# Placing the feature-tile sum of a projection in a later step of a fused spectral and attention kernel

## The chip, the cores and the metric

The kernel runs on one core of one Trainium2 chip. The metric is the device time of one execution in microseconds (us), the median of several runs; the profile comes from one execution of its own. Engines are named as in the profile: PE is TensorE (PEld its weight loads), DVE is VectorE, ACT is ScalarE, POOL is GpSimd, SP issues most of the DMAs.

## The reference

Four layers, each added to a residual of 2048 rows by 512 columns, each behind a layer norm: a Fourier mixing layer (real part of a transform along the hidden axis and then along the sequence), an attention layer with memory, and the same two again. The attention layer has 32 heads of 16 columns and goes over the sequence in four segments of 512 rows:

```python
phi = lambda t: jnp.where(t > 0, t + 1.0, jnp.exp(t))
for s in range(N):
    qs, ks, vs = q[:, :, s], k[:, :, s], v[:, :, s]
    logits = jnp.einsum("bhqd,bhkd->bhqk", qs, ks) * scale + mask
    p = _softmax(logits, axis=-1)
    a_dot = jnp.einsum("bhqk,bhkd->bhqd", p, vs)
    pq = phi(qs)
    num = jnp.einsum("bhld,bhde->bhle", pq, M)
    den = jnp.einsum("bhld,bhd->bhl", pq, z)[..., None] + 1e-6
    a_mem = num / den
    o = g * a_mem + (1.0 - g) * a_dot
    outs.append(o)
    pk = phi(ks)
    M = M + jnp.einsum("bhld,bhle->bhde", pk, vs)
    z = z + jnp.einsum("bhld->bhd", pk)
```

So a feature tile `phi(q)` is wanted in segments 1 to 3 (to read the memory), and `phi(k)` in segments 0 to 2 (to add to it). The mask adds -1e9 where the key lies behind the query.

## The kernel before

The four layers are written as Python generators, one step of each at a time. `place(order, gen, slots...)` puts the steps of a generator on a list of slots; the program is then written slot by slot, within a slot by `order`. In an attention layer a unit is four heads of one segment, 32 units in all, and takes 10 slots; a group `g` is two units (20 slots), a segment four groups. Slot `b` is where a segment's first unit starts, `t` where a group's does.

What stands on an engine's queue is not simply that order. A scheduling layer below puts each engine's instructions in order by readiness and priority: TensorE's stay in the order written (`keep_in_program_order`), instructions under `tc.high_priority` go earlier, and `tc.issue_after(x)` (in the helper `after`) holds an instruction back behind `x` in that order. Waits between engines are then derived from the data.

The steps that matter here:

- `proj(s, g, n)` (from line 996) makes the projection of `q` or `k` of one group: 12 matmuls `pqk` in four steps. In the fourth, ScalarE copies the result to `praw` (line 1032), GpSimd splits off the bf16 parts (`parts` line 1033, `rem` line 1034), and `feature()` puts two ScalarE passes down, relu (line 1024) and exp (line 1025), into the tile `phi`. The next step is ScalarE's second part (line 1038) and, before the change, `feature_sum()`: one VectorE instruction (line 1029) that reads `praw` and `phi` in SBUF, 128x512 f32 each, and writes the finished `phi`. Then GpSimd's third part (line 1042) and the DMAs to DRAM. For groups 0 and 1 of segment 0 (`late`) both `feature()` and the sum come in a step of their own instead.
- `natural_max(s, g, u)` makes a unit's scores row by row (matmuls `nat<-stkk,stkq`) and reduces each to its maximum by one VectorE instruction and a read of its accumulator (line 1102, `junk` and `mx`): 32 pairs a unit, 1024 in the program, written with high priority. Lines 1118 to 1125 split the maxima into bf16 parts (`mparts`), which TensorE turns (`mT`).
- `softmax_values` makes the scores again transposed (`sT`), subtracts the maxima in the same matmul, and ScalarE applies relu and exp into `pT` (lines 1175 and 1176); GpSimd zeroes the future by a select (line 1181); `pv_bank` matmuls follow, and `output` scales them on VectorE (lines 1268 to 1288) and adds the memory's part on GpSimd (line 1286).
- `nat`, `sT`, `pqk`, `pvv`, `po` and the rest take their PSUM from one ring of seven banks (`bank`). A matmul that opens a bank waits for whoever read what was there seven banks earlier, which is VectorE for a bank of `nat`.
- `mem_read` (matmuls `pm`) and `mem_update` (transposes `pkT`) are the readers of `phi`. They stand on slots that come 17 or more behind the sum's step.

Where the steps stood:

```python
yield
A.activation(parts[:, 1], rem, AF.Copy)
if with_phi and not late:
    feature_sum()
yield
E.tensor_tensor(out=parts[:, 2], in0=rem, in1=parts[:, 1], op=ALU.subtract)
```

with the four steps of the matmuls on four slots `at`, and the rest on `post(at[3])`, the three slots behind the last of them.

Of the kernel before, what the change touches and what calls it, by code (L numbers as in the profile page):

```python
# [58 lines left out]
def spectral_infini_kernel(  # L59
# [11 lines left out]
    folded=None,  # L71
):
    nc = tc.nc
    V, A, G, T = nc.vector, nc.scalar, nc.gpsimd, nc.tensor
# [78 lines left out]
        G.tensor_tensor(out=r[:n], in0=ve[:n], in1=half_neg[:n], op=ALU.pow)  # L153
        return mv, ve, r

    first_row, opened, drained = [], [], []

    @contextmanager
    def after(what):
        with ExitStack() as all_:  # L160
            for i in what:
                all_.enter_context(tc.issue_after(i.ins))
            yield
# [36 lines left out]
    def place(order, gen, *at):  # L200
        for t in itertools.chain(*at):
            slots.setdefault(t, []).append((order, gen))
# [735 lines left out]
    def place_attention(x_in, x_out, t0, ws, w_at, out_at, last=None, final=False, turned=False):  # L938
# [59 lines left out]
        def proj(s, g, n):  # L998
            ps = bank("pqk")
            for d in range(DT):  # L1000
                matmul3(
                    ps,
                    lambda h: ws[n, d][:, h, g * P : (g + 1) * P],
                    lambda h: xT[s][:, h, d, :],
                    d == 0,
                    d == DT - 1,
                )
                if d + 1 < DT:
                    yield

            def phi_tile():
                if (s, g) not in phi:
                    phi[s, g] = pair("phi", "ut", 8, F32)
                return phi[s, g][:, "qk".index(n)]

            parts = sb.tile([P, 3, 512], BF16, name="parts", bufs=2)
            with_phi = (n == "q" and s > 0) or (n == "k" and s < NSEG - 1)
            late = s == 0 and g < 2
            rem = sb.tile([P, 512], F32, name="rem", bufs=1)
            raw = sb.tile([P, 512], F32, name="praw", bufs=2) if with_phi else rem  # L1020
            sign = -1.0 if n == "q" else 1.0

            def feature():
                A.activation(phi_tile(), raw, AF.Relu, scale=-sign)
                A.activation(phi_tile(), phi_tile(), AF.Exp, scale=-1.0)

            def feature_sum():
                op = (ALU.min, ALU.subtract) if n == "q" else (ALU.max, ALU.add)
                V.scalar_tensor_tensor(phi_tile(), raw, 0.0, phi_tile(), op0=op[0], op1=op[1])

            E = V if turned and (s, g) == (0, 0) else G
            A.activation(raw, ps, AF.Copy, scale=sign)
            E.tensor_copy(parts[:, 0], raw)
            E.tensor_tensor(out=rem, in0=raw, in1=parts[:, 0], op=ALU.subtract)
            if with_phi and not late:
                feature()
            yield
            A.activation(parts[:, 1], rem, AF.Copy)  # L1038
            if with_phi and not late:
                feature_sum()  # L1040
            yield
            E.tensor_tensor(out=parts[:, 2], in0=rem, in1=parts[:, 1], op=ALU.subtract)  # L1042
            yield
            sd = dram.tile([NSLOT, P, 512], BF16, name=f"scr{n}", bufs=3)
            dst = sd.rearrange("o p s -> p o s")
            o = 0
            for a, cnt, step in SLOTS[n]:
                src = parts[:, a : a + cnt] if step else parts[:, a : a + 1].to_broadcast(
                    [P, cnt, 512]
                )  # L1050
                nc.sync.dma_start(dst[:, o : o + cnt], src)
                o += cnt
            scr[s, g, n] = sd
            yield
            if with_phi and late:
                feature()
                feature_sum()
                yield

        def stack(s, g, u):  # L1060
# [19 lines left out]
        def natural_max(s, g, u):  # L1080
            qs, ks = stacks[s, g, u, "q"], stacks[s, g, u, "k"]
            mx = sb.tile([P, HU, LT], F32, name="mx", bufs=2)

            def scores(*cols):
                ps = bank("nat")
                views, off = [], 0
                for h, i in cols:
                    n = (i + 1) * P
                    T.matmul(
                        ps[:, off : off + n],  # L1090
                        qs[:KROWS, h, i * P : (i + 1) * P],
                        ks[:KROWS, h, :n],
                        start=True,
                        stop=True,
                    )
                    views.append((ps[:, off : off + n], mx[:, h, i : i + 1]))
                    off += n
                for src, dst in views:
                    n = src.shape[1]
                    junk = sb.tile([P, 512], BF16, name="junk", bufs=1)  # L1100
                    with tc.high_priority(offset=URGENT):
                        V.tensor_tensor_reduce(  # L1102
                            junk[:, :n], src, mask[:, 512 - n :], 1.0, 3e38,
                            ALU.add, ALU.min, dst,
                        )

            for h in range(HU):
                scores((h, 3))
                yield
                scores((h, 0), (h, 2))  # L1110
                yield
                if h % 2:
                    scores((h - 1, 1), (h, 1))
                    yield
            parts = max_parts[((s * NG + g) * (HG // HU) + u) % 2]
            rem = sb.tile([P, HU, LT], F32, name="mrem", bufs=2)
            with tc.high_priority(offset=2 * URGENT):
                V.scalar_tensor_tensor(
                    parts[:, 0], mx, -2.0, mx, op0=ALU.mult, op1=ALU.add
                )  # L1120
                for dst in rem, parts[:, 1]:
                    V.scalar_tensor_tensor(
                        dst, mx, -1.0, parts[:, 0], op0=ALU.mult, op1=ALU.subtract
                    )
                V.scalar_tensor_tensor(
                    parts[:, 2], rem, 1.0, parts[:, 1], op0=ALU.mult, op1=ALU.subtract
                )
            maxima[s, g, u] = parts
            yield
# [324 lines left out]
        def post(t):  # L1454
            return [t + 1, t + 2, t + 3]
# [6 lines left out]
        for n in range(NSEG * USEG):  # L1462
            t = t0 + SU * n
# [11 lines left out]
        for s in range(NSEG):  # L1475
# [27 lines left out]
            for g in range(NG):  # L1503
                t = b + SG * g
                late = [] if s or g > 1 else [b + 3 + 2 * g]
                at = {
                    (0, 0): [b - FOLD + 27 + k // 2 for k in range(8)] if turned else run_from(b - 34, 8),
                    (0, 1): run_from(b - 18, 8),
# [2 lines left out]
                    (1, 0): among(b - 40, b - 29, 8),  # L1511
                    (1, 1): among(b - 29, b - 17, 8),
                }.get((s, g), light(t - 50))
                place(2, proj(s, g, "q"), at[:4], post(at[3]))
                place(2, proj(s, g, "k"), at[4:], post(at[7]), late)
                if s > 0:
                    place(2, mem_read(s, g), [t - 12, t - 8])
                if s < NSEG - 1:
# [43 lines left out]
    else:  # L1562
# [11 lines left out]
        for t, (edge, other) in zip(folded.masks, ((0.0, 1.0), (0.0, -1.0))):  # L1574
# [15 lines left out]
            late=taken,  # L1590
# [210 lines left out]
```

## Time and profile before

| what | value |
|---|---|
| median of 3 runs | 1245.22 us (1245.03 to 1257.96) |
| time of the profiled execution | 1242.76 us |
| its span, first to last instruction | 1241.0 us |
| mean granted TensorE clock | 0.983 |
| PE busy | 1149.4 us, 93% |
| DVE busy | 952.8 us, 77% |
| ACT busy | 850.1 us, 68% |
| POOL busy | 433.8 us, 35% |
| sums of line 1029 | 48, 44.4 us in all |

The first attention layer fills the span from about 110 us to 620 us, the second from about 720 us on; the stretches before them are the Fourier layers. In a row of the timeline stand the start in us, the duration in us, engine, line, operation, what is written and read, and in brackets the idle time of the engine just before and what ended it. In a row of the waits stand who waited for whom, the total in us, how often, and the longest.

### The profile page before, as it was taken

The page shows a single profiled execution, that of the slowest core. Times are in us where ns is not written, and L with a number is a line of the kernel's source. Part 1 is how long each engine was busy: PE and PEld are TensorE (multiplying, and loading weights), DVE is VectorE, ACT ScalarE, POOL GpSimd, SP SyncE. Part 2 cuts the span into 40 slices and gives each one's busy share as a digit, 9 for nine tenths or more (in the row PEclk, how much of TensorE's full clock was granted, in tenths as well). Part 3 has the DMA queues.
Part 4 walks back from the last instruction along what each step waited for, and adds up shares of the span by engine and source line. Part 5 has one row for each costly group of instructions (what it writes and reads, how often), then busy time and mean ns, then how long its engine had stood idle before and what let it go on. Part 6 is the DMA issues. An engine that isn't in the chain of part 4 may idle for free.

```text
span 1241.0 us, 24436 instructions
## 1 busy us (share of the span) xinstructions
PE 1149.4 (93%) x7720; PEld 743.6 (60%) x7720; DVE 952.8 (77%) x3440; ACT 850.1 (68%) x1928; POOL 433.8 (35%) x750
## 2 busy tenths in 40 slices
PE   6989898998999999988989998899999999999897
PEld 5766455666655665545577764556666556655454
DVE  8788787778877877777697787877787778777772
ACT  5463487887787777886525426888777887878762
POOL 1111453433444444441110134454334443435200
PEclk9999898999999999998999998999999999999999
DMA  9596544435554454462428773543354444544411
GB/s 367 179 307 224 171 141 122 142 121 159 162 158 120 136 174 133 139 207 91 154 84 272 271 248 123 157 136 123 106 178 155 139 137 143 162 140 135 151 45 54
DMA packets 111125, 197.66 MB, mean 159 GB/s; under 512 B 13917, under 2 KB 63075, under 8 KB 110986
## 3 DMA queue, kind: packets, MB, share of 16 engines
q1 hardware_dynamic: 107722, 195.22, 49.0%
q8 instruction: 63, 1.03, 0.3%
q10 hardware_dynamic: 3264, 0.79, 0.3%
q14 instruction: 76, 0.62, 0.2%
HBM read 128.04 MB, written 67.14 MB: 157 GB/s over the span
## 4 chain that ended last, share of the span: by engine, by line
PE 61%; DVE 16%; DMA 7%; ACT 7%; issue 5%; POOL 3%; SPq 0%; ACTq 0%; DVEq 0%; POOLq 0%
PE pqk L85 11%; PE pv_bank L85 9%; PE sT L85 8%; PE nat L85 8%; DVE junk L1102 7%; PE u L85 5%; PE po L85 5%; PE pvv L85 5%; DMA chk<-in_chk 4%; ACT pT L1176 2%; PE pm L85 2%; PE pM L85 2%; PE on L85 1%; ACT sT L1175 1%; PE yr L85 1%
## 5 line engine op out<-in xcount | busy, mean ns | idle before, releaser
L1102 DVE CUSTOM_DVE_ANT_0 junk<-nat,mask 128x512 bf16<-128x512 f32 (+3 forms) x1024 | 500.2, 489 | 141.8 <-PE nat L85 108.2
L1176 ACT ACTIVATE pT<-sT 128x512 f32<-128x512 f32 x640 | 367.0, 598 | 45.0 <-PE sT L85 20.3
L1181 POOL TENSOR_SCALAR_AFFINE_SELECT pT<-pT 128x512 f32<-128x512 f32 x392 | 169.8, 446 | 404.0 <-ACT pT L1176 364.9
L85 PE MATMUL sT<-stkq,stkk 99*128 99x256 bf16 (+3 forms) x1024 | 250.4, 308 | 15.9 <-DVE mx L1102 9.8
L85 PE MATMUL nat<-stkk,stkq 96*128 96x512 bf16 (+3 forms) x1024 | 237.2, 303 | 20.4 <-DVE mx L1102 17.7
L1175 ACT ACTIVATE sT<-sT 128x256 f32<-128x256 f32 (+1 forms) x560 | 182.5, 335 | 55.7 <-PE sT L85 49.7
L85 PEld LDWEIGHTS <-stkk 99*128 99x128 bf16 x1024 | 83.2, 99 | 140.8 <-issue 125.5
L85 PE MATMUL pv_bank<-pT,vt 128*17 128x512 f32 (+3 forms) x2048 | 151.5, 434 | 0.0
L85 PEld LDWEIGHTS <-stkq 96*128 96x128 bf16 x1024 | 92.7, 99 | 65.8 <-issue 26.4
L85 PE MATMUL pqk<-xT,wq 128*128 128x512 f32 x384 | 126.2, 441 | 3.3 <-ACT xT L100 1.8
L85 PE MATMUL pqk<-xT,wk 128*128 128x512 f32 x384 | 126.6, 442 | 0.3
L85 PE MATMUL pvv<-wv,xT 128*128 128x512 f32 x384 | 122.0, 432 | 2.0 <-DVE mx L1102 2.0
L85 PE MATMUL po<-wo,oh 128*128 128x512 f32 x384 | 121.7, 435 | 2.2 <-DVE oh L102 1.4
L904 ACT ACTIVATE chk<-chk,reps 128x1024 f32<-128x1024 f32 (+1 forms) x80 | 81.4, 1022 | 40.1 <-DMA chk<-in_chk 39.8
L85 PEld LDWEIGHTS pv_bank<-pT,vt 128*17 128x17 f32 x2048 | 53.3, 97 | 79.4 <-issue 75.2
L1286 POOL TENSOR_TENSOR onat<-onat,otmp 128x128 f32<-128x128 f32 x96 | 48.5, 513 | 103.8 <-DVE otmp L1285 97.8
L1102 DVE DVE_READ_ACCUMULATOR2_ANT mx<- 128x1 f32 x1024 | 84.1, 82 | 0.0
L1042 POOL TENSOR_TENSOR parts<-rem,parts 128x512 bf16<-128x512 f32 x60 | 72.4, 1207 | 27.9 <-ACT parts L1038 23.1
L85 PEld LDWEIGHTS po<-wo,oh 128*128 128x128 f32 x384 | 68.6, 193 | 21.4 <-DVE oh L102 3.6
L85 PEld LDWEIGHTS pqk<-xT,wq 128*128 128x128 f32 x384 | 69.2, 191 | 16.2 <-ACT xT L100 2.3
L85 PEld LDWEIGHTS pqk<-xT,wk 128*128 128x128 f32 x384 | 68.8, 195 | 13.6 <-DVE mx L1102 1.0
L85 PEld LDWEIGHTS pvv<-wv,xT 128*128 128x128 f32 x384 | 67.4, 189 | 15.6 <-DVE mx L1102 4.5
(257 smaller groups left out, 1671.7 us busy)
## 6 DMA issues: line engine op xcount, KB each, us to landing
chk<-in_chk SPq DMA_DIRECT2D x68, 512.0 KB
stkq<-scrq SPq DMA_DIRECT2D x64, 384.0 KB
stkk<-scrk SPq DMA_DIRECT2D x64, 384.0 KB
scrq<-parts SPq DMA_DIRECT2D x32, 384.0 KB
scrk<-parts SPq DMA_DIRECT2D x32, 384.0 KB
mid<-xrm SPq DMA_DIRECT2D x32, 256.0 KB
scrq<-parts SPq DMA_DIRECT2D x32, 256.0 KB
scrk<-parts SPq DMA_DIRECT2D x32, 256.0 KB
```

What stands on the lines that cost most here:

```text
L85: return tc.keep_in_program_order(op(*args, **kwargs))
L904: A.activation(t[:, c : c + row], t[:, c : c + row], AF.Abs, bias=rep[:, col : col + 1], scale=scale, accum_out=acc[:, col : col + 1],)
L1042: E.tensor_tensor(out=parts[:, 2], in0=rem, in1=parts[:, 1], op=ALU.subtract)
L1102: V.tensor_tensor_reduce(junk[:, :n], src, mask[:, 512 - n :], 1.0, 3e38, ALU.add, ALU.min, dst,)
L1175: A.activation(blocks, blocks, AF.Relu)
L1176: A.activation(dst, ps, AF.Exp, scale=-SCALE)
L1181: G.affine_select(blocks, blocks, pattern=[[0, n] for n in blocks.shape[1:-1]] + [[1, P]], compare_op=ALU.is_ge, fill=0.0, base=0, channel ...
L1286: G.tensor_tensor(out=dst, in0=dst, in1=tmp, op=ALU.add)
```

## The change

The sum is taken out of the projection's fifth step and gets one of its own at the end, five slots behind the last matmuls (`end`) rather than one, for all 22 sums of an attention layer that are not `late`. In it, `after(last_max)` holds it behind the maximum that was written last at that point. `numerators` is declared and not used.

```diff
-    first_row, opened, drained = [], [], []
+    first_row, opened, drained, numerators, last_max = [], [], [], [], []
...
             A.activation(parts[:, 1], rem, AF.Copy)
-            if with_phi and not late:
+            if with_phi and not late and not folded:
                 feature_sum()
...
             if with_phi and late:
                 feature()
                 feature_sum()
+                yield
+            elif folded:
+                if with_phi:
+                    with after(last_max):
+                        feature_sum()
                 yield
...
-                        V.tensor_tensor_reduce(
+                        last_max[:] = [V.tensor_tensor_reduce(
                             junk[:, :n], src, mask[:, 512 - n :], 1.0, 3e38,
                             ALU.add, ALU.min, dst,
-                        )
+                        )]
...
+                end = lambda t: [t + 5] if turned and (s or g > 1) else []
...
-                place(2, proj(s, g, "q"), at[:4], post(at[3]))
-                place(2, proj(s, g, "k"), at[4:], post(at[7]), late)
+                place(2, proj(s, g, "q"), at[:4], post(at[3]), end(at[3]))
+                place(2, proj(s, g, "k"), at[4:], post(at[7]), end(at[7]), late)
```

The order of instructions on PE, ACT and SP is the same before and after. On POOL some of the additions of line 1286 stand behind one or two selects more. On DVE the 44 sums stand 6 to 20 rows further down, and some neighbours (`xn`, `xT`, `oh`, `xo`) trade places with a maximum. Behind line 1057 the lines of the changed kernel have numbers that are 5 higher, so its maxima are line 1107.

First place: VectorE's queue at the projection of `q` of the third group of segment 2 in the first attention layer (the sum that runs at 381 us in the profile). Before, the sum stands ahead of the pairs that follow it:

```order
L1029 SCALAR_TENSOR_TENSOR phi<-praw,phi 128x512
L1102 ISA junk,mx<-nat,mask 128x256
L1102 ISA mx 128x1
L1102 ISA junk,mx<-nat,mask 128x256
L1102 ISA mx 128x1
L1102 ISA junk,mx<-nat,mask 128x512
L1102 ISA mx 128x1
L1102 ISA junk,mx<-nat,mask 128x128
L1102 ISA mx 128x1
L1102 ISA junk,mx<-nat,mask 128x384
L1102 ISA mx 128x1
```

The same stretch now:

```order
L1107 ISA junk,mx<-nat,mask 128x256
L1107 ISA mx 128x1
L1107 ISA junk,mx<-nat,mask 128x256
L1107 ISA mx 128x1
L1107 ISA junk,mx<-nat,mask 128x512
L1107 ISA mx 128x1
L1107 ISA junk,mx<-nat,mask 128x128
L1107 ISA mx 128x1
L1107 ISA junk,mx<-nat,mask 128x384
L1107 ISA mx 128x1
L1029 SCALAR_TENSOR_TENSOR phi<-praw,phi 128x512
```

The sum went behind five maxima, ten rows.

Second place: the landing of the sum for `k` of the same group, before (the sum stood 15 rows higher):

```order
L1125 SCALAR_TENSOR_TENSOR mparts_75<-mrem,mparts_75 128x16
L1102 ISA junk,mx<-nat,mask 128x512
L1102 ISA mx 128x1
L1268 RECIPROCAL rec<-on 128x16
L1102 ISA junk,mx<-nat,mask 128x128
L1102 ISA mx 128x1
L1269 TENSOR_TENSOR rec<-rec,gate 128x16
```

and now:

```order
L1130 SCALAR_TENSOR_TENSOR mparts_75<-mrem,mparts_75 128x16
L1107 ISA junk,mx<-nat,mask 128x512
L1107 ISA mx 128x1
L1273 RECIPROCAL rec<-on 128x16
L1029 SCALAR_TENSOR_TENSOR phi<-praw,phi 128x512
L1107 ISA junk,mx<-nat,mask 128x128
L1107 ISA mx 128x1
L1274 TENSOR_TENSOR rec<-rec,gate 128x16
```

The sum now stands right ahead of a maximum, behind the reciprocal that scales the unit before.

Third place: the landing of the sum for `q` of segment 1's last group (it runs at 282 us before and stood 17 rows higher). Before:

```order
L1102 ISA junk,mx<-nat,mask 128x128
L1102 ISA mx 128x1
L1102 ISA junk,mx<-nat,mask 128x384
L1102 ISA mx 128x1
L177 TENSOR_SCALAR xn<-xt,norms,roots 128x512
L1102 ISA junk,mx<-nat,mask 128x512
```

and now:

```order
L1107 ISA junk,mx<-nat,mask 128x384
L1107 ISA mx 128x1
L1029 SCALAR_TENSOR_TENSOR phi<-praw,phi 128x512
L177 TENSOR_SCALAR xn<-xt,norms,roots 128x512
L1107 ISA junk,mx<-nat,mask 128x512
```

The sum now stands ahead of `xn`, a row of the next segment's normalised input.

## The prediction

> **What bounds the kernel now.** I read the page first, then who TensorE waits for, then the two attention layers as windows, and last the sums themselves. From the page, the span, the busy times and the chain that ended last:
>
> ```profile
> span 1241.0 us, 24436 instructions
> PE 1149.4 (93%) x7720; PEld 743.6 (60%) x7720; DVE 952.8 (77%) x3440; ACT 850.1 (68%) x1928; POOL 433.8 (35%) x750
> PE 61%; DVE 16%; DMA 7%; ACT 7%; issue 5%; POOL 3%; SPq 0%; ACTq 0%; DVEq 0%; POOLq 0%
> ```
>
> TensorE is the bound, and where the chain leaves it, it goes through VectorE more than twice as often as through ScalarE. TensorE's idle time is what a change that leaves its work alone can win. Its waits, over the whole span:
>
> ```profile
> PE nat L85 <- DVE mx L1102: 17.7, 35, 1.2
> PE sT L85 <- DVE mx L1102: 9.8, 18, 1.2
> PE on L85 <- ACT ot L1249: 6.3, 6, 1.8
> PE pM L85 <- DVE mx L1102: 3.5, 4, 0.9
> PE pvv L85 <- DVE mx L1102: 2.0, 6, 0.4
> ```
>
> The maxima (`mx`) end most of them: a matmul wants a bank of the ring whose maximum has not been taken. The first attention layer as one window (length, then busy time of each engine) shows how much there is:
>
> ```profile
> 150.00:600.00 450.00, 423.50 (x2996) 260.70 (x2995) 351.50 (x1405) 351.46 (x826) 185.35 (x321) 0.98 0.45 141
> ```
>
> TensorE is idle for 450.00 - 423.50 = 26.5 us there. VectorE has 98.5 us of idle time, so it is late only at places, not as a whole. The sums, as a line and as a group:
>
> ```profile
> L1029 DVE SCALAR_TENSOR_TENSOR phi<-praw,phi x48: 647/855/1640, 109.6 to 1141.6; 128x512 f32<-128x512 f32 x48
> L1029 DVE SCALAR_TENSOR_TENSOR phi<-praw,phi 128x512 f32<-128x512 f32 x48 | 44.4, 925 | 8.8 <-ACT phi L1025 8.3
> ```
>
> A sum takes 0.65 us at best, 1.64 at worst, and VectorE stands still for 8.3 us in all until ScalarE's exp is done. One of them from close by, in the order of time:
>
> ```profile
> 281.73 0.63 ACT L1025 ACTIVATE phi<-phi 128x512 f32<-128x512 f32 x1
> 281.95 1.16 POOL L1034 TENSOR_TENSOR rem<-praw,parts 128x512 f32<-128x512 f32 x1
> 282.38 1.28 DVE L1029 SCALAR_TENSOR_TENSOR phi<-praw,phi 128x512 f32<-128x512 f32 x1 [1.18 <-ACT phi L1025]
> 284.52 0.38 PE L85 MATMUL sT<-stkq,stkk 99*128 99x512 bf16 x1 [0.32 <-DVE mx L1102]
> 285.57 0.38 PE L85 MATMUL nat<-stkk,stkq 96*128 96x512 bf16 x1 [0.67 <-DVE mx L1102]
> 286.83 1.16 PE L85 MATMUL pM<-vt,pkn 128*128 128x136 f32 x8 [0.88 <-DVE mx L1102]
> ```
>
> VectorE waits 1.18 us for exp, then the sum takes 1.28, twice its best. The maxima queue behind it for 2.46 us, and TensorE stands still three times, 0.32 + 0.67 + 0.88 = 1.87 us, each time for a maximum.
>
> **What goes: the stalls at the old places.** I looked in the first layer for TensorE's waits within some 3 us behind each of the 22 sums that move, and kept those ended by VectorE. There are 16, in 9 places: the three above, the same three at 412.73, 413.77 and 415.03, and ten more, the first, some between and the last of which are, with the one left out at 186.97 and the last of the second layer,
>
> ```profile
> 185.55 0.38 PE L85 MATMUL sT<-stkq,stkk 99*128 99x384 bf16 x2 [0.65 <-DVE mx L1102]
> 186.97 0.38 PE L85 MATMUL nat<-stkk,stkq 96*128 96x256 bf16 x2 [0.80 <-DVE mx L1102]
> 323.40 0.38 PE L85 MATMUL nat<-stkk,stkq 96*128 96x128 bf16 x2 [0.46 <-DVE mx L1102]
> 384.07 0.97 PE L85 MATMUL pvv<-wv,xT 128*128 128x512 f32 x3 [0.36 <-DVE mx L1102]
> 510.99 0.97 PE L85 MATMUL pvv<-wv,xT 128*128 128x512 f32 x3 [0.36 <-DVE mx L1102]
> 540.31 0.97 PE L85 MATMUL po<-wo,oh 128*128 128x512 f32 x3 [0.22 <-DVE oh L102]
> 1144.79 0.96 PE L85 MATMUL po<-wo,oh 128*128 128x512 f32 x3 [0.23 <-DVE oh L102]
> ```
>
> By place they come to 0.65 + 1.87 + 0.86 + 0.36 + 1.87 + 0.22 + 0.28 + 0.36 + 0.46 = 6.9 us. (The 0.80 at 186.97 is that of an `xn` that stands between, and stays.) At each place what the sum holds VectorE for is more than the gap, so the whole gap can go. The second layer has the same waits 605 us later, the last at 1144.79 (0.23), so 13.8 us in all. Behind the other 13 sums that move TensorE waits for no maximum of theirs.
>
> **What comes: the sums at the new places.** A sum is now ready long before its turn, so the wait for exp goes, and each costs its own 0.65 to 1.64 us less the room there: VectorE's idle time up to the next maximum that a matmul is waiting for. At 16 of 22 places there is room enough, since VectorE waits for `nat` anyway. Two such places, where the sum now comes ahead of a maximum that had waited:
>
> ```profile
> 355.53 0.69 DVE L1102 CUSTOM_DVE_ANT_0 junk<-nat,mask 128x512 bf16<-128x512 f32 x1 [0.77 <-PE nat L85]
> 541.77 0.69 DVE L1102 CUSTOM_DVE_ANT_0 junk<-nat,mask 128x512 bf16<-128x512 f32 x1 [0.71 <-PE nat L85]
> ```
>
> At six places a layer there is little. As windows from the new place to that next maximum (length, PE, PEld, DVE busy):
>
> ```profile
> 190.07:193.28 3.21, 2.78 (x22) 1.92 (x20) 3.01 (x14) 3.21 (x10) 0.95 (x2) 1.00 0.05 12
> 290.08:292.38 2.30, 1.99 (x14) 1.54 (x13) 2.07 (x5) 2.30 (x6) 1.55 (x3) 1.00 0.42 147
> 298.91:300.05 1.14, 0.91 (x7) 0.59 (x6) 1.14 (x8) 1.14 (x5) 0.15 (x1) 1.00 0.54 205
> 331.95:333.07 1.12, 1.12 (x6) 0.43 (x5) 1.11 (x6) 0.73 (x4) 0.62 (x2) 1.00 0.00 0
> 391.58:392.53 0.95, 0.95 (x5) 0.43 (x5) 0.94 (x7) 0.04 (x1) 0.00 (x0) 1.00 1.02 370
> 418.29:420.35 2.06, 1.98 (x14) 1.55 (x13) 1.82 (x4) 1.93 (x5) 1.32 (x2) 1.00 0.19 66
> ```
>
> VectorE's idle time in them is 0.20, 0.23, 0, 0.01, 0.01 and 0.24, together 0.69 us. Six sums at 0.65 cost 3.90 - 0.69 = 3.2 us a layer; six at 1.64 cost 9.84 - 0.69 = 9.2. I take the short price. The long one is that of a sum beside GpSimd's part of a projection:
>
> ```profile
> 292.23 1.16 POOL L1042 TENSOR_TENSOR parts<-rem,parts 128x512 bf16<-128x512 f32 x1 [0.75 <-ACT parts L1038]
> 292.30 1.64 DVE L1029 SCALAR_TENSOR_TENSOR phi<-praw,phi 128x512 f32<-128x512 f32 x1
> 418.29 1.16 POOL L1034 TENSOR_TENSOR rem<-praw,parts 128x512 f32<-128x512 f32 x1
> 418.53 1.21 DVE L177 TENSOR_SCALAR xn<-xt,norms,roots 128x512 f32<-128x512 f32 x1 [0.23 <-PE xnT L85]
> ```
>
> The sum at 292.30 ends 0.55 us after GpSimd's instruction does, as does the one at 282.38. Four of the six places have at most short selects beside them. At the other two, ahead of `xn` (290.08 and 418.29), `rem` runs, but there `xn` waits for it already, so a sum that waits out the same instruction adds its own 0.55 to 0.65 rather than the wait once more.
>
> The Trainium skill, page “SBUF — State Buffer”, section “Who interferes with whom”, says that a VectorE instruction with two inputs in SBUF and a GpSimd one that reads SBUF shut each other out for a whole instruction, whoever comes first. The trace agrees (1.64 us beside a GpSimd instruction of 1.16). By the rule the new places are no safer than the old where a later `rem` has just begun, so it speaks against the change; a sum would then cost up to 1.16 + 0.65 = 1.81 us, an estimate, and six of them 10.2 us a layer.
>
> Costed at nothing: the bookkeeping of `last_max` issues no instruction. The later end of `phi` is covered by the 17 slots or more to its readers, of which the move takes four; were that gone, `pm` or `pkT` would wait. `praw` has two buffers and is kept four slots longer; the next projection that wants the same one is a whole projection further. The queues of SP and ACT keep their order, and the additions on GpSimd (line 1286) that trade places with selects have 65% of idle time on that engine about them.
>
> **The sum.** 13.8 - 2 x 3.2 = 7.4 us of TensorE's idle time go. Not all of it reaches the end: a TensorE that is earlier meets what is late next, and that is ScalarE (`on <- ot` above, and its share of 7% in the chain). I take the ratio of the chain, 7 of 7 + 16, for what is given back: 30%, leaving 5.2 us. Against the profiled execution's own 1242.8 that is 1237.6; the median of the runs shown is 2.4 us higher, 1245.2, so I forecast **1240 us**.
>
> **The rivals.**
>
> *Given back whole* (1245 us). TensorE's order is unchanged and ScalarE is busy for 351.46 of 450 us in the window, as much as VectorE. If the banks that ScalarE reads (`sT`) are as late as those of `nat`, each gap reappears one matmul on. Against it: in the row of waits `mx` ends 17.7 + 9.8 us and `ot`, the first of ScalarE's, 6.3. The same time comes out if the change does not do what it says, that is if the gaps are those of `nat` and `xn` and not of the sums; the three rows from 284.52 on speak against that.
>
> *All of it* (1231 us). The gaps go whole and the new places cost nothing, because everything ahead of them is earlier too: 1245.2 - 13.8 = 1231.4. For it: the VectorE that is 2.46 us earlier at 282 has more room at 290. Against it: a TensorE that is earlier by as much takes that room away.
>
> *Long sums at the tight places* (1250 to 1264 us). The sums land on GpSimd's instructions at all six places and last 1.64 us: 2 x 9.2 = 18.3 us of new stalls, less 13.8 gives 1249.7; less half of it, if ScalarE is late next, 1256.6; less nothing, 1263.5. It decides slower by over 1% (1257.7) from where less than 5.8 of the 13.8 us are won. For it: the median sum is 0.855, not 0.65, and `rem` is at two of the places. Against it: four of the six have no `rem` or `parts` within a sum's length. The skill's page above names the mechanism; the price is the row's.
>
> **How the numbers follow.** Forecast 0.52 (its own range 1236 to 1244: 9.2 down to 1.2 us won), given back whole 0.22 (1243 to 1248), all of it 0.14, long sums 0.12. About 1%, 12.4 us, is what a measurement of this kernel can tell from no change. Faster by over 1% is “all of it”: 0.14. Slower by over 1% is the worse half of “long sums”: 0.06. The rest, 0.80, lies within. The range runs from all of it, 1231, to the best of the long sums, 1249; it leaves out the worse long sums and what lies under 1231.
>
> **What would show it.** Right: the idle time before line 1029 falls from 8.8 us to under 1; TensorE's waits at the old places (the three from 284.52, the three from 412.73) are gone; waits of `nat` and `sT` for `mx` fall from 27.5 us to about 20; sums that are not beside `rem` or `parts` take 0.65 to 0.69 us. New waits of 0.4 to 0.7 us stand behind the six places. Wrong: the sums' mean stays above 0.9 us, or TensorE's waits for `ot`, `pT` and `mt` grow by as much as those for `mx` fall, or TensorE's busy time falls or grows by more than the waits do.

## The result and the profile after

| | median | runs |
|---|---|---|
| before | 1249.13 us (1242.07 to 1260.24) | 22 |
| changed | 1241.69 us (1237.14 to 1249.64) | 22 |
| ratio | 0.994, 95% interval 0.9921 to 0.9959 | |

The change wins 7.4 us, 0.6%: less than the 1% taken as the bound for "no change", but not nothing, since the interval ends below 1. The median of the kernel before is 4 us higher over these 22 executions than over the three that the prediction started from, so the ratio is the better number: 0.994 of 1245.2 is 1237.7.

The profiled execution of the changed kernel seems to say the opposite. Its page:

```profile
span 1244.8 us, 24443 instructions
PE 1157.8 (93%) x7720; PEld 749.3 (60%) x7720; DVE 953.1 (77%) x3440; ACT 850.3 (68%) x1928; POOL 435.2 (35%) x750
PE 67%; DVE 13%; ACT 7%; DMA 5%; issue 5%; POOL 4%; SPq 0%; POOLq 0%; DVEq 0%; ACTq 0%
```

The span is 3.8 us longer than before and TensorE 8.4 us busier with the same 7720 matmuls. Most of that comes from a stretch of the first Fourier layer, which the change doesn't touch. The same window in both kernels, before first (start and end, length, busy time of PE, PEld, DVE, ACT, POOL, then the granted clock):

```profile
66.80:80.50 13.70, 13.70 (x66) 9.95 (x65) 11.27 (x30) 9.98 (x18) 1.78 (x5) 1.00 0.93 319
```

```profile
66.80:80.50 13.70, 13.70 (x31) 8.50 (x31) 6.89 (x20) 6.77 (x13) 1.10 (x2) 0.50 0.65 237
```

TensorE is busy all the time in both, but at a granted clock of 0.50 it gets 31 matmuls done instead of 66. Every trace here has dips to 0.50, most of them of 3.4 or 6.8 us. Shorter ones come back at nearly the same times (near 150, 200, 755 and 805 us); this long one, 13.7 to 20.5 us at 67 us, is in five of the fourteen traces (the changed kernel, `e1`, `e2`, `f1`, `g3`) and not in the other nine, `f2` and `h1` among them. So two profiles are compared below from the same matmul to the same matmul (TensorE's order is the same in all kernels), and where the clock is 1.00 in both. Most of the first attention layer, from matmul 1200 to matmul 2880, is such a stretch; before, then after:

```profile
233.32:481.72 248.40, 239.25 (x1687) 152.51 (x1680) 195.44 (x757) 196.12 (x459) 106.81 (x186) 1.00 0.46 143
```

```profile
237.54:482.35 244.81, 237.46 (x1688) 152.20 (x1680) 194.99 (x755) 196.24 (x460) 106.73 (x186) 1.00 0.47 145
```

It takes 3.6 us less: half of the 7 us, in one of the two layers. TensorE's idle time goes from 9.15 to 7.35 us, and its busy time falls by as much, 1.8 us, though the matmuls and the clock are the same.

The sums and TensorE's waits in the changed kernel:

```profile
L1029 DVE SCALAR_TENSOR_TENSOR phi<-praw,phi x48: 627/686/1076, 116.1 to 1150.6; 128x512 f32<-128x512 f32 x48
L1029 DVE SCALAR_TENSOR_TENSOR phi<-praw,phi 128x512 f32<-128x512 f32 x48 | 34.7, 724 | 0.0
```

```profile
PE nat L85 <- DVE mx L1107: 16.1, 32, 1.4
PE on L85 <- ACT ot L1254: 9.1, 7, 2.9
PE sT L85 <- DVE mx L1107: 7.0, 12, 1.7
PE pvv L85 <- ACT mt L1145: 4.0, 2, 2.1
PE pM L85 <- DVE mx L1107: 3.5, 4, 0.9
```

VectorE no longer waits in front of the sums (8.8 us before, 8.3 of it for exp; now 0.0), and the 48 sums take 34.7 us instead of 44.4. But VectorE's busy time is the same in both kernels, mainly because the small instructions that split the maxima take 60.8 us instead of 49.9. The two that grow most, before and after:

```profile
L1118 DVE SCALAR_TENSOR_TENSOR mparts<-mx 128x16 bf16<-128x16 f32 x64 | 14.7, 229 | 2.1
L1122 DVE SCALAR_TENSOR_TENSOR mrem<-mx,mparts 128x16 f32<-128x16 f32 x64 | 13.3, 208 | 1.8
```

```profile
L1123 DVE SCALAR_TENSOR_TENSOR mparts<-mx 128x16 bf16<-128x16 f32 x64 | 20.5, 321 | 2.0
L1127 DVE SCALAR_TENSOR_TENSOR mrem<-mx,mparts 128x16 f32<-128x16 f32 x64 | 17.4, 272 | 1.8
```

One of them in the changed kernel, at 128x16 a thirty-second of the sum's size and 0.17 us at the median, lasts 1.17 beside a GpSimd instruction that began 0.02 us earlier:

```profile
360.03 1.17 POOL L1042 TENSOR_TENSOR parts<-rem,parts 128x512 bf16<-128x512 f32 x1 [0.74 <-ACT parts L1038]
```

```profile
360.05 1.17 DVE L1123 SCALAR_TENSOR_TENSOR mparts<-mx 128x16 bf16<-128x16 f32 x1
```

So other VectorE instructions now meet GpSimd: 28 of the 256 splits last over 0.5 us, 9 before. This does not set the time: in the runs below the splits take 59.2 us with the sums left out (`e4`, 14 us faster than before) and 51.3 with only the q sums moved (`e2`, as fast as the whole change).

The waits of `nat` and `sT` for a maximum fall from 27.5 to 23.1 us, those of `pvv` are gone, and those of `pM` are as they were. The waits for ScalarE grow, those for `ot` by 2.8 us and those for `mt` by 3.0; all of TensorE's waits for ScalarE together go from 16.3 to 21.1 us.

The place that the prediction showed, in the changed kernel:

```profile
287.60 0.94 PE L85 MATMUL pqk<-xT,wk 128*128 128x512 f32 x3
288.38 0.39 PE L85 MATMUL sT<-stkq,stkk 99*128 99x512 bf16 x1
288.83 0.38 PE L85 MATMUL nat<-stkk,stkq 96*128 96x512 bf16 x1
290.09 1.17 PE L85 MATMUL pM<-vt,pkn 128*128 128x136 f32 x8 [0.88 <-DVE mx L1107]
```

Of the three waits there the first two (0.32 and 0.67) are gone; the third, 0.88 before `pM`, stands as it stood. In the kernel before, the last of those three matmuls stood alone ahead of the wait:

```profile
283.81 0.40 PE L85 MATMUL pqk<-xT,wk 128*128 128x512 f32 x1
```

From its start to the start of `sT` at 284.52 are 0.71 us, where three of them in the changed kernel take 288.38 - 287.60 = 0.78, 0.26 each. The wait, listed as 0.32, cost 0.45: a matmul that is followed at once overlaps with the next, and one that is followed by a wait doesn't. A loss of this kind is in the busy time; how much of the 1.8 us it makes up is not shown. The Trainium skill, page “Perfetto Trace Analysis”, section “Tensor Engine Instruction (MATMUL, LD_WEIGHTS)”, says that the end of a matmul in a trace is computed, not observed. No run here shows that by itself; starts are the safer thing to compare, and here they give the larger loss.

### The profile page after: what moved, and what is told of

It reads as the page before. It is cut to its first block, busy times and chain, and to the rows that moved or that the text cites. A ratio compares the mean times of both kernels' runs of the same rounds, so it can differ in the third digit from the quotient of the medians.

```text
span 1244.8 us, 24443 instructions
## 1 busy us (share of the span) xinstructions
PE 1157.8 (93%) x7720; PEld 749.3 (60%) x7720; DVE 953.1 (77%) x3440; ACT 850.3 (68%) x1928; POOL 435.2 (35%) x750
## 4 chain that ended last, share of the span: by engine, by line
PE 67%; DVE 13%; ACT 7%; DMA 5%; issue 5%; POOL 4%; SPq 0%; POOLq 0%; DVEq 0%; ACTq 0%
PE pqk L85 12%; PE pv_bank L85 10%; PE sT L85 9%; PE nat L85 8%; PE u L85 7%; PE pvv L85 5%; DVE junk L1107 5%; PE po L85 5%; DMA chk<-in_chk 3%; ACT pT L1181 2%; PE pm L85 2%; PE yr L85 2%; PE pM L85 2%; PE on L85 2%; ACT sT L1180 1%
## 5 line engine op out<-in xcount | busy, mean ns | idle before, releaser
L1186 POOL TENSOR_SCALAR_AFFINE_SELECT pT<-pT 128x512 f32<-128x512 f32 x392 | 174.3, 458 | 406.6 <-ACT pT L1181 365.0
L85 PE MATMUL pvv<-wv,xT 128*128 128x512 f32 x384 | 126.9, 445 | 4.0 <-ACT mt L1145 4.0
L85 PEld LDWEIGHTS po<-wo,oh 128*128 128x128 f32 x384 | 67.2, 190 | 23.1 <-DVE oh L102 4.3
L85 PEld LDWEIGHTS pvv<-wv,xT 128*128 128x128 f32 x384 | 70.5, 196 | 17.5 <-ACT mt L1145 4.6
L1291 POOL TENSOR_TENSOR onat<-onat,otmp 128x128 f32<-128x128 f32 x96 | 43.3, 459 | 99.1 <-DVE otmp L1290 98.2
```

Source lines behind the costliest of these rows:

```text
L85: return tc.keep_in_program_order(op(*args, **kwargs))
L1186: G.affine_select(blocks, blocks, pattern=[[0, n] for n in blocks.shape[1:-1]] + [[1, P]], compare_op=ALU.is_ge, fill=0.0, base=0, channel ...
L1291: G.tensor_tensor(out=dst, in0=dst, in1=tmp, op=ALU.add)
```

## The experiments

Each of 235 executions lists its span and its mean granted clock. Within one kernel the span grows by 0.97 us for each 0.001 that the clock is lower (fitted over all of them). The column "span at 0.979" is the mean of the spans, each corrected by that to a clock of 0.979; it separates the kernels better than the medians do.

| run | median us | ratio, 95% interval | span at 0.979 | to before |
|---|---|---|---|---|
| before (92 executions) | 1248 to 1250 | 1 | 1247.1 | |
| changed | 1241.69 | 0.9940 (0.9921 to 0.9959) | 1240.0 | -7.1 |
| e1: changed, again | 1240.27 | 0.9944 (0.9911 to 0.9977) | 1240.1 | -7.0 |
| e2: only the q sums moved | 1242.10 | 0.9950 (0.9920 to 0.9980) | 1239.9 | -7.2 |
| e3: only the k sums moved | 1250.82 | 1.0021 (0.9994 to 1.0048) | 1247.0 | -0.1 |
| e4: the 44 sums left out | 1233.82 | 0.9891 (0.9852 to 0.9930) | 1233.0 | -14.1 |
| f1: q sums moved, k sums left out | 1237.63 | 0.9898 (0.9853 to 0.9942) | 1236.3 | -10.8 |
| f2: k sums two steps later still | 1239.67 | 0.9919 (0.9890 to 0.9948) | 1238.6 | -8.5 |
| f3: weight checks later | 1242.60 | 0.9942 (0.9912 to 0.9973) | 1243.2 | -3.9 |
| f4: f2 and f3 | 1241.74 | 0.9940 (0.9909 to 0.9970) | 1240.4 | -6.7 |
| g1: changed, weight checks without loads | 1228.20 | 0.9847 (0.9799 to 0.9896) | 1230.9 | -16.2 |
| g2: before, weight checks without loads | 1237.04 | 0.9916 (0.9878 to 0.9954) | 1237.4 | -9.7 |
| g3: q sums two steps earlier | 1250.36 | 0.9997 (0.9968 to 1.0027) | 1246.6 | -0.5 |
| h1: f2 with the weight checks held | 1241.34 | 0.9942 (0.9917 to 0.9967) | 1241.7 | -5.4 |

The standard error of a corrected span is 0.2 to 0.8 us.

Two edits were not run because they can't change anything: the new step without the hold, and the hold at the old step, each give every engine the same order of instructions as before. It takes both to move a sum.

### Which sums the gain comes from

The change once more, as the measure of what repeats:

> The changed kernel once more, for a second profile beside the others on the same chip. All theories: 0.994 of the kernel before. What differs between its two profiles at the same instruction is not the change's: the first one fell behind by 8.0 us between 46 and 88 us, in a Fourier stage whose instructions are the same; if that was the granted clock of that execution it will not come again at that place. The wait of 1.9 us for ScalarE's copy of the turned maxima (`pvv` for `mt`) near 395 us should come again, if it is the chain behind a check's load.

The time repeats (0.9944), and so does the wait near 395 us (1.82 us, at 401 in this trace). The dip does too, against the expectation: 20.5 us from 66.6 us on.

Then half of it. In `e2` the k sums stay in the old step, in `e3` the q sums do:

```diff
-            if with_phi and not late and not folded:
+            if with_phi and not late and not (folded and n == "q"):
                 feature_sum()
...
-                if with_phi:
+                if with_phi and n == "q":
                     with after(last_max):
```

> Only the sums for q are moved, those for k stay. Theory (the gain is TensorE's waits at the old places, the cost the tight new places): 6.3 of the 6.9 us of waits a layer stand behind sums for q, and two of the six tight places are theirs (0.83 us), so 5.4 us net a layer; two layers, less 30%: 7.6 us, 0.994, as good as the whole change or up to 2.5 us better. Rival (what counts is VectorE's time, 9.7 us less in line 1029, shared by both kinds alike): 20 of 44 sums, so a little under half of the gain, 0.997.

> Only the sums for k are moved. Theory: 0.65 us of waits a layer go and four tight places come (2.4 us), so 1.7 us a layer lost; two layers, less 30%: 2.4 us slower, 1.002. Rival (VectorE's time): a little over half of the gain, 0.997.

And the ceiling: the folded kernel without the 44 sums, so that `phi` of those groups holds only the exponential:

```diff
             elif folded:
-                if with_phi:
-                    with after(last_max):
-                        feature_sum()
+                pass
                 yield
```

> The 44 sums are left out (phi stays without the linear part, so the memory reads and writes something else): the most that any place for them can win. Theory: the 13.8 us go and no new place costs anything, less 30% that meet ScalarE or a load: 9.7 us, 0.992. Rival (after the first few us a wait for ScalarE or a check's load ends later than VectorE anyway): no better than the changed kernel, 0.994. If it is under 0.990, VectorE bounded more than the 16 waits counted.

The q sums bring the whole gain (0.995, 7.2 us corrected) and the k sums none (1.002). The rival of both runs, 0.997 each, is out: the interval of `e3` begins at 0.9994. Without any sum 14 us go, about twice the gain: 0.9891 is below the 0.992 expected, and 14.1 us corrected is the 13.8 of the theory with no 30% taken off. The stretch from matmul 1200 to 2880, with only the q sums moved and with no sums:

```profile
241.39:485.48 244.09, 237.73 (x1687) 152.04 (x1680) 194.55 (x758) 196.31 (x460) 105.68 (x187) 1.00 0.46 145
```

```profile
230.19:472.80 242.61, 236.88 (x1688) 152.18 (x1680) 186.62 (x741) 195.91 (x459) 102.80 (x186) 1.00 0.46 146
```

244.09 against 248.40 before and 244.81 with all sums moved: the same answer from single profiles. Leaving the sums out makes it 242.61.

What stays of TensorE's waits for maxima when there are no sums at all:

```profile
PE nat L85 <- DVE mx L1105: 12.3, 26, 1.2
PE sT L85 <- DVE mx L1105: 7.1, 13, 1.7
PE pM L85 <- DVE mx L1105: 3.5, 4, 0.9
```

The four waits of `pM`, 0.9 us each, are there too. They never belonged to the sums.

### What a sum costs at which place

A unit makes 16 maxima (1024 over the 64 units of both layers; the "32 pairs a unit" in the account of the kernel is wrong). In most groups the q sum of the changed kernel stands behind the eleventh maximum of a group's second unit, the k sum behind the first of a unit. In the trace without sums VectorE stood idle, over the seventh to the 28th unit of each layer, for 462 ns on average ahead of the maximum that follows the q place, and for 78 ns ahead of the one that follows the k place (the 26 ns of the expectation are those of the same place in a group's other unit). If a place costs what its idle time doesn't cover, the k sums pay and the q sums don't.

```diff
-                if with_phi:
+                if with_phi and n == "q":
                     with after(last_max):
```

> The q sums in the fifth step as in the changed kernel, the 20 moved k sums left out (their sum is missing from the result). Theory: the q sums stand ahead of the third 512-column maximum of a pair of units, where VectorE idled 462 ns on average in the run without sums, so they cost almost nothing there; the k sums stand behind the first maximum of a unit, where it idled 26 ns, so what was left between the changed kernel and the run without sums is theirs: ratio to before about 0.990, 1236 us, close to the run without sums (0.989). Rival: both kinds share what is left: about 0.992, 1238 to 1239 us.

```diff
-                place(2, proj(s, g, "k"), at[4:], post(at[7]), end(at[7]), late)
+                place(2, proj(s, g, "k"), at[4:], post(at[7]), end(at[7] + 2), late)
```

> The changed kernel with the k sums two steps later still, behind the fourth maximum of a unit in most units. Theory (a place costs what the idle time of VectorE there doesn't cover): ahead of the fifth maximum VectorE idled 636 ns on average in the run without sums, so the k sums go too: ratio about 0.991, 1237 us. Rival (the idle time of VectorE is no room, since TensorE works on the next scores in it and is late by the same amount): unchanged at 0.994 to 0.996, 1241 to 1243 us.

The third moves the q sums two steps up, to the eighth maximum of the second unit (not the sixth, as the expectation says; the maximum behind it is the one of 512 columns that it names):

```diff
-                place(2, proj(s, g, "q"), at[:4], post(at[3]), end(at[3]))
+                place(2, proj(s, g, "q"), at[:4], post(at[3]), end(at[3] - 2))
```

> The changed kernel with the q sums two steps earlier, behind the sixth maximum of the second unit of a pair instead of the eleventh-to-last place they have now, that is ahead of the next 512-column maximum, where VectorE idled 289 ns on average in the run without sums (at the place of the change 462 ns). Theory (the price of a place is what its idle time doesn't cover): 24 sums by 0.65 - 0.29 = 0.36 us is 8.7 us against 24 by 0.19 = 4.6 us: 4 us slower than the changed kernel, 0.997, 1244 us. Rival (what the old place cost was the wait for the exponential and GpSimd's use of the memory there, and both are over by this step): as the changed kernel, 0.994, 1240 us.

From the corrected spans, for both layers together: the 20 k sums cost 1239.9 - 1236.3 = 3.6 us at the old place, 1240.1 - 1236.3 = 3.8 at the new one, and 1238.6 - 1236.3 = 2.3 two steps further (`f2`). The 24 q sums cost 1236.3 - 1233.0 = 3.3 us at the new place, 3.3 + 7.0 = 10.3 at the old one, and 3.3 + 6.5 = 9.8 in `g3`. Each of these costs has a standard error of 0.8 to 1.1 us, most of it from the six executions of `f1`. So in `f1` the rival is right: its median fits the first theory's number (1237.6 for 1236), but what is left above the run without sums is shared, 3.3 and 3.8 us, and the roomy q place is not free. Per sum that is 0.14 us for q, 0.19 for k, and 0.12 for k two steps later (636 ns of idle time), all much less than the 0.65 us a sum takes; the differences among the three are within their errors. `f2` goes the way of the theory, and no further than half of what it gave. `g3` goes its way too, but lost not 4 us: all of the gain went. Its sums:

```profile
L1029 DVE SCALAR_TENSOR_TENSOR phi<-praw,phi x48: 627/687/1647, 116.9 to 1155.3; 128x512 f32<-128x512 f32 x48
L1029 DVE SCALAR_TENSOR_TENSOR phi<-praw,phi 128x512 f32<-128x512 f32 x48 | 41.3, 860 | 0.0
```

The median is that of the changed kernel (686), the mean isn't: 41.3 us in all instead of 34.7. VectorE waits for no exp there. Some sums are twice as long; one from close by, in the order of time:

```profile
327.81 1.17 POOL L1042 TENSOR_TENSOR parts<-rem,parts 128x512 bf16<-128x512 f32 x1 [0.32 <-ACT parts L1038]
...
327.88 1.65 DVE L1029 SCALAR_TENSOR_TENSOR phi<-praw,phi 128x512 f32<-128x512 f32 x1
...
330.18 0.22 PE L85 MATMUL nat<-stkk,stkq 96*128 96x128 bf16 x1 [1.07 <-DVE mx L1107]
```

GpSimd's subtraction of the same projection began 0.07 us earlier, and the sum ends 0.55 us after it does; a `nat` then waits 1.07 us for a maximum. So the rival's "both are over by this step" was wrong for GpSimd: the step is not late enough to be clear of it. In the Trainium skill, page “SBUF — State Buffer”, section “Who interferes with whom”, the first of two such instructions to be issued keeps a port that VectorE shares with GpSimd for its whole length, and the other waits. The trace agrees nearly: the sum ends 0.55 us after GpSimd's instruction, and takes 0.63 alone.

Over the same 70 matmuls about the sum, TensorE is 1.0 to 1.24 us slower than in the changed kernel at each of the five sums that last over 1.6 us, 5.8 us together; at the other nineteen q sums it is 0 to 0.41 us slower, 3.0 us together. Some of that is made up later, since the whole loss is 6.5 us. The long sums are the larger part of it; that the rest is the smaller room at the place is not shown. And since VectorE waits for no exp in `g3` and nothing is won, the 8.3 us of waiting for exp are not by themselves what the change wins.

`f2`, 0.9919, is the fastest kernel here that computes everything, 1.4 us (two standard errors) below the changed kernel in corrected spans. By medians alone the two can't be told apart.

### Was part of the gain given back to ScalarE?

The waits for ScalarE grew. One of the longest, in the changed kernel, ScalarE first and then TensorE (before, the wait there was 1.00 us, of the `sT` three matmuls further):

```profile
393.91 1.15 ACT L904 ACTIVATE chk<-chk,reps 128x1024 f32<-128x1024 f32 x1 [0.68 <-DMA chk<-in_chk]
...
395.36 0.26 ACT L1145 ACTIVATE mt<-mT 48x128 bf16<-48x128 bf16 x1
...
395.67 0.50 PE L85 MATMUL pvv<-wv,xT 128*128 128x512 f32 x1 [1.90 <-ACT mt L1145]
```

ScalarE takes a block of weights (a weight check: 512 KB from DRAM, summed) that has not landed; the copy `mt`, which frees a bank for `pvv`, stands behind it in ScalarE's queue. TensorE's waits of over 0.5 us that end on a copy just behind such a block come to 12.2 us in the changed kernel's attention layers and 5.9 us before (the expectations below put them at about 10 and 4). `f3` was to move the work away from its load:

```diff
-            return [t, t + 3]
+            return [t, t + (3 if n < early else 5)]
```

> The changed kernel with the weight checks taken on ScalarE two steps later behind their loads, in the attention stages; nothing left out. In the changed kernel about 10 us of TensorE's waits in the attention stages end on ScalarE copies that stand behind a check whose load had not landed (before: about 4 us). Theory (what the sums gave was in part given back here): 4 to 6 us faster than the changed kernel, ratio to before about 0.990, 1236 us. Rival (TensorE makes these waits up within a unit, since the other engines run ahead meanwhile): as the changed kernel, 0.994, 1240 to 1242 us.

> Both edits: k sums two steps later and the checks two steps later; nothing left out. Theory: the gains add, ratio about 0.987, 1232 us. If only one of the two acts, 0.990 to 0.991; if neither, 0.994.

Neither gained anything: `f3` is 3.2 us slower than the changed kernel in corrected spans, `f4` 1.8 slower than `f2`. But they don't decide: in the order that came of it the work stands only 0 to 8 instructions further down ScalarE's queue, mostly 0 to 3, and the waits for the loads are still there. So the loads themselves went, in the changed kernel and in the kernel before:

```diff
-            nc.sync.dma_start(t, src)
+            loaded = k % per_half < 20
+            if loaded:
+                nc.sync.dma_start(t, src)
...
-                        t[:, c : c + row], t[:, c : c + row], AF.Abs,
+                        t[:, c : c + row].rearrange("p (a b) -> p a b", b=P),
+                        t[:, c : c + row].rearrange("p (a b) -> p a b", b=P)
+                        if loaded
+                        else folded.flip.unsqueeze(1).to_broadcast([P, row // P, P]),
+                        AF.Abs,
...
```

(Not shown: the results for these blocks go into a spare column.)

> The changed kernel with the 28 weight checks that run beside attention taken over a small resident tile instead of a loaded one: ScalarE does the same work, but the loads (512 KB each) and the waits for their landing are gone, and these 28 blocks of weights are not checked. In the changed kernel about 10 us of TensorE's waits end on ScalarE copies that stand behind such a check, in the kernel before about 4 us. Theory (part of what the sums gave was given back there): about 6 us faster than the changed kernel, ratio to before 0.989, 1235 us, and more than the same edit gives the kernel before (next run). Rival (a wait at a check is made up for within the unit, so nothing was given back there): as much or as little as in the kernel before, 0.992 to 0.994 if that is 0 to 2 us.

> The kernel before with the same 28 checks taken over a resident tile; the 28 blocks of weights are not checked. Theory of the give-back: 2 to 3 us faster than before, ratio 0.998, so that the distance to the changed kernel with the same edit grows from 7 to 10 us. Rival: the distance stays at 7 us.

Both kernels get some 9 us faster (corrected: 9.1 and 9.7), and the distance between them stays: 1237.4 - 1230.9 = 6.5 us with the edit, 7.1 without, each with an error of 0.4 to 0.6. (By the medians, in which the clock is not taken out, it is 8.8 against 7.4.) This is the rival's case in what matters, though not in size: it had put the saving at 0 to 2 us. These loads cost the kernel before as much as the changed one, although the lists show 6 us more of waits behind them in the changed one.

The last run keeps the loads and holds the work back instead, behind the last exponential put down (`last_exp`), with the later step of `f3` and the k sums of `f2`:

```diff
-                A.activation(dst, ps, AF.Exp, scale=-SCALE)
+                last_exp[:] = [A.activation(dst, ps, AF.Exp, scale=-SCALE)]
...
-                with after((opened, drained[:1], drained[1:2])[min(k // 2, 2)] if k < 20 else ()):
+                with after((opened, drained[:1], drained[1:2])[min(k // 2, 2)] if k < 20 else last_exp if k % per >= 20 else ()):
```

> All sums as in the run with the k sums two steps later still, and each of the 28 weight blocks summed on ScalarE beside attention held behind the last exponential put down, in a step two later than now: about 15 instructions of ScalarE further behind its load, which is issued where it was; nothing left out. Theory (the 9 to 10 us that went with the loads were waits for their landing): the block has landed when ScalarE comes to it, 5 to 9 us less than without the hold, ratio about 0.987, 1232 us. Rival (they were the traffic of the loads, or the place of this work among ScalarE's copies): as without the hold, 0.992, 1239 us, or slower.

TensorE's waits in it:

```profile
PE nat L85 <- DVE mx L1109: 12.2, 28, 1.2
PE sT L85 <- DVE mx L1109: 10.5, 21, 1.5
PE pv_bank L85 <- POOL pT L1188: 5.6, 6, 1.3
PE sT L85 <- DMA stkq<-mt: 5.5, 9, 1.0
PE on L85 <- ACT ot L1256: 1.3, 2, 0.7
PE sT L85 <- ACT mt L1147: 0.8, 1, 0.8
```

The waits for `ot`, 8.4 us in `f2` and 9.1 in the changed kernel, are down to 1.3, those for `mt`, 3.4 and 4.7, to 0.8, and the time is no better: 1241.3 us, corrected 3.1 us more than `f2`. The work came to stand 2 to 10 instructions further down, not 15, but ScalarE waits for none of these blocks any more. The rival has the time right, but the run does not show that the waits at the landings were worth nothing, since the hold brings others in their place: `pv_bank` for GpSimd's select `pT`, 5.6 us (no such row in `f2`), and `sT` for the DMA of `stkq`, 5.5 us (2.2). TensorE's listed waits come to about 78 us in both. Counted over the same matmuls where the clock is 1.00 in both, `h1` is 4.2 us faster than `f2` at the eight places where ScalarE waited for a block in `f2` (100 matmuls each), and 11.1 us slower at seven others (160 matmuls, 1.1 to 2.0 us each). The traces of `g2` and of the kernel before say the same of the loads: at the six places where ScalarE waited for a block and the clock allows the comparison, `g2` is 7.3 us faster. So most of the 9.7 us that went with the loads in that kernel went where they landed late. What the rest was, the traffic or something else, was not separated.

## Why the prediction held, and where it didn't

1240 us was forecast and 1241.7 measured, with "within 1%" at 0.80. The ratio, 0.994, is a gain of 7 us against the 5.2 that were worked out. That the time came so close is in part luck: the kernel before ran 4 us slower here, and the change won 2 us more. Point by point:

- *VectorE's places, not its sum of work, are what costs.* Held. VectorE's busy time hardly changes (952.8 and 953.1 us; what the sums lose, the splits of the maxima gain), and where 24 sums stand decides 7 us.
- *What goes, 13.8 us.* The total is close to the 14.1 us that go when the sums are left out, but errors cancel in it. By kind, 12.6 us were to go with the q sums and 1.3 with the k sums (6.3 and 0.65 a layer); measured are 10.3 and 3.6. "At each place what the sum holds VectorE for is more than the gap, so the whole gap can go" failed for `pM`: its four waits of 0.88, 3.5 of the 13.8 us, are in every trace, with no sums too (longer in that of `g3`). That a wait stands behind a sum, and is shorter than it, does not make it the sum's. On the other side a wait that goes takes more with it than its listed length (0.45 for 0.32 above), which the prediction left out; whether this alone makes up the difference is not shown.
- *What comes, 3.2 us a layer.* 6.4 us for both, against 1240.1 - 1233.0 = 7.1 measured. By kind, the six places were to cost the q sums 2 x (1.30 - 0.47) = 1.7 us and the k sums 2 x (2.60 - 0.22) = 4.8; measured are 3.3 and 3.8. So the total is better than its parts. The short price fits the sums' length, 0.69 us at the median, and behind the two places ahead of `xn` there are the waits foretold, 0.58 to 0.59 us each. Behind the other four, all of k sums, no wait for a maximum is listed. One of the two, in the changed kernel:

```profile
296.15 0.27 PE L85 MATMUL nat<-stkk,stkq 96*128 96x256 bf16 x1 [0.59 <-DVE mx L1107]
```

- *30% given back.* This step failed. The sum before it, 13.8 - 6.4 = 7.4 us, is what was measured. The waits for ScalarE did grow, by 4.8 us, but `g1` and `g2` show that the largest of them, those at the loads, cost the kernel before as much as the changed one, and `e4` won the whole 14.1 us. Whether something was given back elsewhere and made up by the part of a wait that no list shows, these runs can't tell. The chain's share, 7 of 7 + 16, was no measure here for what the gain would lose.
- *The sign to look for:* `nat` and `sT` for `mx` to about 20 us; they are at 23.1. The two that would have spoken against the theory both happened, waits for `ot` and `mt` that grow by as much as those for `mx` fall and a busy time that grows by 8.4 us, and neither meant what the prediction said: the first is told above, and the second goes with the clock, since the busy time falls where the clock is 1.00 in both.
- *Rivals.* "Given back whole" is out: the interval ends at 0.9959. "All of it" would take places that cost nothing; 14.1 us is what it would be worth. "Long sums" did not happen at the new places (1.08 us at most, 724 ns on average), but it is a real mechanism two steps earlier: in `g3` it cost most of the gain.

## What to carry to other kernels

When an instruction that is off the critical path holds up a queue on it, move it to where that queue waits anyway, and look at each kind of instruction by itself: here 24 sums won everything, 20 nothing, and the same 24 two steps earlier nothing either, mainly because some of them meet a GpSimd instruction there. A list of waits shows where to look but is no price list: waits that stood behind a sum were not its own, and a hold that took 9 us of waits for ScalarE away brought as many for GpSimd and the DMA. To price a wait, leave the work out that is thought to cause it, and compare from one instruction to the same instruction, at the same clock.

## What was not expected of the hardware

- TensorE's granted clock falls to 0.50 for 13.7 us with TensorE busy throughout, at 67 us in five of fourteen traces and not in the others. Over 235 executions a mean clock lower by 0.001 goes with 0.97 us more; that is most of the scatter within a kernel (in the kernel before 4.5 us of standard deviation, 1.9 when corrected), and the 12.5 us between the fastest and the slowest execution of the changed kernel are more than the effect studied.
- A wait of TensorE can cost more than its listed idle time, since the matmul ahead of it loses its overlap with the next: 0.45 us for a listed 0.32 at the place shown.
- VectorE's instructions of 128x16 that take 0.17 us at the median take up to 1.17 beside a GpSimd instruction. When the sums moved away from GpSimd, these took 11 us more in all.
- 28 loads of 512 KB that run beside attention cost some 9 us of 1240, most of it, in the kernel before, where a load landed late. That is more than the change won. It is the next thing to look at in this kernel.
